# Keys as the moving operand, exp(S) as the stationary one, in a decode-attention and MLP kernel

## The chip, the cores and the metric

The kernel runs on one core of a Trainium2 chip. The metric is device time in microseconds (us), the median of several executions. A run is called slow when it lies over 1.5% above the fastest run of the same kernel. PE is TensorE's matmuls, PEld its weight loads, DVE VectorE, ACT ScalarE, POOL GpSimd, SP the engine that issues the loads. The granted clock is the share of TensorE's full clock that the profile records as let through; half clock is a share of 0.5.

## The reference

One decode step for four sequences: attention over a window of 2048 cached keys and values, and an MLP branch on the same input. Cut to what matters:

```python
# B=4, D=576, Hq=32, Hkv=16, Dh=128; the last W=2048 of 8192 cached positions
xn = layernorm(x)
q  = xn @ wq                                            # 576 x 4096
s  = einsum(q, k_cache[:, :, -W:]) * Dh**-0.5           # two query heads share one K/V head
o  = einsum(softmax(s), v_cache[:, :, -W:]) @ wo        # 4096 x 576
... # B: x1 = xn + (shifted gelu branch; with S=1 the shift leaves zeros)
h2 = gelu(layernorm(x1) @ w3) @ w4                      # 576 x 4608, 4608 x 576
out = x + o + x1 + h2
```

All inputs are bf16. The kernel must read 87.17 MB from HBM: 16 heads with 2.10 MB of K and 2.10 MB of V each, and wq, wo, w3 and w4.

## The kernel before

For each K/V head it loads K and V whole. VectorE transposes K in 32x32 blocks, four calls a head. TensorE then takes the transposed keys as the stationary operand (loaded into the array) and streams the queries past them. V is the stationary operand of P*V. The eight columns are four sequences times two query heads.

```python
def k_scores(h, s):                       # a quarter of a head: 4 groups x 4 matmuls of 32 columns
    kt = kts.pop((h, s))[:].bitcast(BF16)
    for g in range(SC // NQD):
        for ie in range(4):
            nc.tensor.matmul(out=S_ps[h][:, ...], lhsT=kt[:, ib, ...], rhs=qz[:, h, ib, e]..., ...)

def pv(h, s):                             # 16 matmuls of 8 columns, V stationary, and 2 of ones for the sums
    for g in range(CG):
        nc.tensor.matmul(out=O_ps[h][:, 0:NJ], lhsT=vn[:, g * NQD + s, :], rhs=pt[:, g, s, :], ...)
    ...

for t in range(Hkv):                      # hm = t-1: softmax; hv = t-2: P*V
    for s in range(NSL):                  # four steps
        k_transpose(t, s)                 # VectorE
        if s == 0: sm_max(hm), o_norm(hv - 1)
        elif s == 2: o_pick(hv - 1)       # VectorE's part of the output projection
        pv(hv, s)
        if s == 0: k_mask(t)
        k_scores(t, s)
        if s == 0: sm_maxT(hm)
        elif s == 1: sm_sub(hm), 16 x sm_exp, o_spread(hv - 1)   # spread: every fourth head
        elif s == 3: o_proj(hv - 1)                              # projection: every fourth head
        if t == G_AT: mlp_g(...)          # MLP-up, at t = 7
    flush_loads()                         # issue the loads whose buffers come free
```

Loads go out in the order of use: wq, K0, K1, K2, V0, K3, V1, K4, V2, w3, K5, and so on, w4 last. A load waits for one of seven K/V buffers.

## Time and profile before

| | before |
|---|---|
| time, median | 215.49 us (215.28 to 215.77) |
| span of the profiled run | 213.3 us |
| read from HBM | 87.17 MB |
| busy: PE, DVE, ACT | 57%, 56%, 33% |

These lines of the page of the kernel before give the span, the granted TensorE clock and the DMA share in 40 slices of equal length (a digit is a tenth), the GB/s of each slice, and two DMA queues with their packets, MB and share of 16 engines' time.

```profile
span 213.3 us, 6449 instructions
PEclk9999999999999999999999999999999999999998
DMA  7999999999999999999999999999999999999970
GB/s 247 433 427 418 436 422 430 436 430 418 442 414 429 436 433 420 438 427 430 427 430 430 421 433 425 433 424 427 432 433 421 425 436 424 430 427 419 423 303 29
q1 hardware_dynamic: 6788, 87.17, 96.3%
q8 instruction: 22, 0.36, 0.6%
```

The loads never pause. The next lines are the end of the chain of waits (start, duration, what): the last K, then w4, then the last 16 matmuls and a copy. Nothing but loads holds the end.

```profile
151.57 31.14 DMA kn<-in_A_k_cache_dram
182.73 26.91 DMA w_sb<-in_B_w_dram
209.68 0.46 PE acc L266 x16
210.16 0.31 DVE fin L489
```

Two groups of matmuls by shape (count, busy us, mean ns of one): 512 columns take 601 ns, 144 columns 298 ns.

```profile
L277 PE MATMUL S<-negbig,ohT 4*128 4x512 bf16 x16 | 9.6, 601 | 0.0
L266 PE MATMUL acc<-w_sb,gT 128*32 128x144 bf16 x144 | 4.7, 298 | 1.7 <-DMA w_sb<-in_B_w_dram 1.6
```

### The profile page before, as it was taken

How to read it: one execution, taken by the hardware profiler on the slowest of the kernel's cores; microseconds unless marked ns; L12 is line 12 of the kernel's file. 1: busy time of each engine (PE TensorE's matmuls, PEld its weight loads, DVE VectorE, ACT ScalarE, POOL GpSimd, SP SyncE). 2: the span in 40 equal slices, each digit the busy share in tenths (PEclk: the TensorE clock that was granted, in tenths of full speed). 3: DMA queues.
4: the chain of work that ended last, by engine and by line, in shares of the span. 5: the costliest groups of instructions: out<-in, count | busy, mean ns of one | idle time of the engine just before them, and what ended most of it. 6: DMA issues, size and time to landing. Idle time of an engine off the chain costs nothing. (4 is left out here: it accounts for less than half of the span.)

```text
span 213.3 us, 6449 instructions
## 1 busy us (share of the span) xinstructions
PE 121.1 (57%) x2893; PEld 95.6 (45%) x2893; DVE 119.2 (56%) x223; ACT 70.4 (33%) x258; POOL 8.1 (4%) x18
## 2 busy tenths in 40 slices
PE   0261256757470017157999477786474704869782
PEld 0260133545360015145899365564453603647671
DVE  4708799867470037348610798895664732956120
ACT  0000003681634002608070035670816250618700
POOL 4600300000000000000000000000000000000000
PEclk9999999999999999999999999999999999999998
DMA  7999999999999999999999999999999999999970
GB/s 247 433 427 418 436 422 430 436 430 418 442 414 429 436 433 420 438 427 430 427 430 430 421 433 425 433 424 427 432 433 421 425 436 424 430 427 419 423 303 29
DMA packets 6822, 87.57 MB, mean 410 GB/s; under 512 B 776, under 2 KB 780, under 8 KB 1292
## 3 DMA queue, kind: packets, MB, share of 16 engines
q1 hardware_dynamic: 6788, 87.17, 96.3%
q8 instruction: 22, 0.36, 0.6%
q14 instruction: 4, 0.03, 0.0%
q10 hardware_dynamic: 8, 0.00, 0.0%
HBM read 87.17 MB, written 0.00 MB: 409 GB/s over the span
## 5 line engine op out<-in xcount | busy, mean ns | idle before, releaser
L314 ACT ACTIVATE pt<-S 32x128 bf16<-32x128 f32 x256 | 68.8, 269 | 90.9 <-issue 55.0
L196 DVE STREAM_TRANSPOSE kt<-kn 128x1024 int32<-128x1024 int32 x64 | 74.6, 1208 | 11.6 <-DMA kn<-in_A_k_cache_dram 11.6
L325 PE MATMUL O<-pt,vn 128*128 128x8 bf16 x1024 | 37.5, 169 | 41.9 <-DMA vn<-in_A_v_cache_dram 40.4
L325 PEld LDWEIGHTS <-vn 128*128 128x128 bf16 x1024 | 34.5, 105 | 49.9 <-DMA vn<-in_A_v_cache_dram 42.1
L285 PE MATMUL S<-qz,kt 128*128 128x32 bf16 x1024 | 39.1, 189 | 25.7 <-DVE kt L196 25.7
L285 PEld LDWEIGHTS <-kt 128*128 128x128 bf16 x1024 | 33.6, 106 | 36.6 <-DVE kt L196 30.9
L299 DVE TENSOR_REDUCE m<-mxT 8x1 f32<-8x128 f32 x16 | 4.4, 277 | 41.0 <-PE mxT L297 41.0
L328 PE MATMUL O<-pt,ones_bf 128*128 128x64 bf16 x128 | 17.1, 226 | 0.0
L314 ACT ACT_TABLE_LOAD x1 | 1.3, 1283 | 33.3 <-DVE mx L292 33.3
L377 PEld LDWEIGHTS <-w_sb 128*128 128x128 bf16 x144 | 11.4, 163 | 0.5 <-issue 0.4
L377 PE MATMUL AB<-ln2T,w_sb 128*128 128x4 bf16 x144 | 11.5, 202 | 0.0
L292 DVE TENSOR_REDUCE mx<-S 128x8 f32<-128x512 f32 x16 | 10.5, 654 | 1.0 <-PE S L285 1.0
L307 PE MATMUL S<-dg,ones_bf 8*128 8x512 bf16 x16 | 9.6, 601 | 0.1
L277 PE MATMUL S<-negbig,ohT 4*128 4x512 bf16 x16 | 9.6, 601 | 0.0
L328 PEld LDWEIGHTS <-ones_bf 128*128 128x128 bf16 x128 | 8.4, 104 | 0.0
L379 PE MATMUL AB<-ln2T,w_sb 128*128 128x4 bf16 x36 | 7.3, 202 | 0.0
L336 DVE TENSOR_REDUCE dn<-O 128x8 f32<-128x64 f32 x16 | 3.3, 209 | 5.5 <-PE O L328 5.5
L384 DVE COPY g_x<-AB 128x144 f32<-128x144 f32 x1 | 0.3, 307 | 10.7 <-PE AB L379 10.7
L297 PE MATMUL mxT<-ident_f,mx 128*8 128x128 f32 x16 | 6.0, 374 | 0.3 <-DVE mx L292 0.3
L379 PEld LDWEIGHTS <-w_sb 128*128 128x128 bf16 x36 | 5.9, 163 | 0.0
L266 PE MATMUL acc<-w_sb,gT 128*32 128x144 bf16 x144 | 4.7, 298 | 1.7 <-DMA w_sb<-in_B_w_dram 1.6
L266 PEld LDWEIGHTS <-gT 128*32 128x32 bf16 x144 | 3.8, 130 | 2.4 <-issue 2.2
(76 smaller groups left out, 68.8 us busy)
## 6 DMA issues: line engine op xcount, KB each, us to landing
kn<-in_A_k_cache_dram SPq DMA_DIRECT2D x16, 2048.0 KB, 29.6
vn<-in_A_v_cache_dram SPq DMA_DIRECT2D x16, 2048.0 KB, 26.9
wo_sb<-in_A_wo_dram SPq DMA_DIRECT2D x4, 1152.0 KB, 29.0
w_sb<-in_B_w_dram SPq DMA_DIRECT2D x2, 2304.0 KB, 32.9
wq_sb<-in_A_wq_dram SPq DMA_DIRECT2D x2, 2048.0 KB, 9.5
w_sb<-in_B_w_dram SPq DMA_DIRECT2D x2, 1440.0 KB, 31.7
w_sb<-in_B_w_dram SPq DMA_DIRECT2D x3, 576.0 KB, 30.4
w_sb<-in_B_w_dram SPq DMA_DIRECT2D x1, 1152.0 KB, 31.7
```

The source lines that it names most:

```text
L196: nc.vector.transpose(out=kt[:], in_=src)
L266: nc.tensor.matmul(out=acc[i * QD:(i + 1) * QD, :], lhsT=lhsT, rhs=rhs[:, i * CW:(i + 1) * CW], start=False, stop=False, skip_group_check= ...
L277: nc.tensor.matmul(out=S_ps[h][:].rearrange("p g k j -> p (g k) j"), lhsT=ohT[:], rhs=nb, start=True, stop=False, skip_group_check=True)
L285: nc.tensor.matmul(out=S_ps[h][:, s * (SC // NQD) + g].rearrange("p k j -> p (k j)"), lhsT=kt[:, ib, g * NQD:(g + 1) * NQD, e:2 * QD:2].re ...
L292: nc.vector.reduce_max(out=mx[:], in_=S_ps[h][:].rearrange("p g k j -> p j (g k)"), axis=AX.X)
L297: nc.tensor.transpose(out=mxT[:], in_=st[h][:], identity=ident_f[:])
L307: nc.tensor.matmul(out=S_ps[h][:].rearrange("p g k j -> p (g k) j"), lhsT=ones_bf[0:NJ, :], rhs=dg, start=False, stop=False, skip_group_ch ...
L314: nc.scalar.activation(out=PT[h][kb * QD:(kb + 1) * QD, :, c4, :], in_=S_ps[h][c4 * QD:(c4 + 1) * QD, :, kb, :], func=ACT.Exp, scale=scale)
L325: nc.tensor.matmul(out=O_ps[h][:, 0:NJ], lhsT=vn[:, g * NQD + s, :], rhs=pt[:, g, s, :], start=(g == 0 and s == 0), stop=False, skip_group ...
L328: nc.tensor.matmul(out=O_ps[h][:, NJ:].rearrange("p (c j) -> p c j", j=NJ), lhsT=ones_bf[:], rhs=pt[:, g:g + DG, s, :], start=False, stop= ...
L377: nc.tensor.matmul(out=g_ps[:, i, :], lhsT=w3[:, j * F + e * (F // 2) + f0:j * F + (e + 1) * (F // 2):NFH], rhs=ln2T[:, j, :], start=False ...
L379: nc.tensor.matmul(out=g_ps[:, i, :], lhsT=w3[:, KJ * F + f0:KJ * F + F // 2:NFH], rhs=ln2T[:, KJ + e, :], start=False, stop=False, skip_g ...
```

## The change

Swap the operands. The queries, placed in a block of zeros, become stationary, and 512 keys at a time stream past them: 16 score matmuls a head instead of 64. exp(S) is turned by VectorE and becomes the stationary operand of P*V, with 512 columns of V moving: 16 matmuls instead of 64, in four column groups of the array. q and MLP-up are made wide in the same way. ScalarE needs one exponential per head instead of 16. The core of the diff:

```diff
-NKV = 7
+NKV = 6
-    CW = D // NQD          # projections in 4 column groups of 144
+    CW = D // 2            # 2 column groups of 288
     def k_scores(h, s):
-        for g in range(SC // NQD):
-            for ie in range(4):
-                nc.tensor.matmul(out=S_ps[h][...], lhsT=kt[...], rhs=qz[:, h, ib, e]...)
+        for ie in range(4):
+            nc.tensor.matmul(out=S_ps[h][:], lhsT=qz[:, z0:z0 + P], rhs=kt[:, ib, :, e:2 * QD:2]..., ...)
+    def sm_turn(h):  nc.vector.transpose(out=PT[h][:], in_=E.pop(h)[:])
+    def sm_den(h):   # row sums: one matmul, then a reciprocal on VectorE
-    def pv(h, s):  ... lhsT=vn[:, g * NQD + s, :], rhs=pt[:, g, s, :]     # 64 + 8 sums a head
+    def pv(h):     ... lhsT=pt[:, c, :], rhs=vn[:, :, c, :]               # 16 a head
+    def o_scale(h):  # ScalarE copies O times 1/sum;  o_turn(h): 4 transposes on TensorE, a reduction
     ...
         for s in range(NSL):
             k_transpose(t, s)
+            if s == 0: sm_max(hm), o_turn(hf), k_mask(t)          # hf = t - 3
             k_scores(t, s)
             if s == 0: sm_maxT(hm)
-            elif s == 1: sm_sub(hm), 16 x sm_exp(hm), o_spread(hv - 1)
-            elif s == 3: o_proj(hv - 1)      # and o_pick at s == 2
+            elif s == 1: sm_sub(hm), sm_exp(hm), o_spread(hf)     # with o_pick inside it
+            elif s == 2: o_proj(hf)
+            elif s == 3: sm_turn(hm), sm_den(hm), pv(hv), o_scale(hv)
```

Where both kernels do a step with different tiles, the cut shows only the call. The setup grows too: q is copied and transposed back, and the zeroed query block is four times as large.

## The prediction

> **What bounds the kernel now.** The loads. The page's queue table gives 87.17 MB from HBM at a busy share of 96.3%; the 40 slices show 418 to 442 GB/s from the second slice to the last but two, with no dip. The chain of waits ends in DMA (35% of the span, PE 2%, DVE 2%): its last links are the last K (landed at 182.7 us), the MLP-down weights (209.6), 0.46 us of matmuls, a 0.31 us copy and about 2.8 us of output. Per head the loads need 4.19 MB, about 9.8 us at 430 GB/s.
>
> **What the change does.** Bytes stay the same. Per head, estimates from durations in the trace:
> - TensorE before: 64 score and 64 P*V matmuls at about 33 ns start to start, 8 sums, mask and subtraction at 0.53 us each: about 6 us.
> - After: 16 score matmuls of 512 columns. The groups by shape give 168 ns for 8 columns, 298 for 144, 602 for 512: 0.83 ns a column. The Trainium skill (TensorE: Matmul & The Clock Gate, Part 1) has 1.2 GHz for an idle array, 2.4 GHz after about 3.4 us of sustained work; this trace shows only the slow rate. The scores are then 6.8 us slow or 3.5 us fast; P*V, four column groups at once, 1.8 or 0.9; mask, subtraction, transposes 1.5 to 2. Sum: 10.3 us slow, 6 us fast: fewer instructions, not less TensorE time. I expect the dense streams to raise the clock at least partly.
> - ACT: 4.3 to about 1.4 us.
> - DVE: the K transposes stay, the turn of exp(S) adds about 0.6 us: 6.4 to about 7 us.
> All this lies off the critical path.
>
> **What could reach the path.**
> 1. Start. The q chain grows: the first K transpose moves from 26.9 us to about 32 (estimate). With six K/V buffers instead of seven, six loads cover the queue until about 45.5 us (summed bytes). The seventh needs the first K released, at about 37 us; the eighth the second K, at about 46, and it is needed by about 48. Probably no gap, else 1 to 3 us.
> 2. End. The final projections use two column groups of 288 in place of four of 144: per weight tile about 240 ns slow, against 130. The last two pieces of MLP-down then end 0.3 to 1.1 us later after the same landing; the split copy returns 0.1.
> 3. Instruction fetch (0.6% of DMA time) shrinks to a third: at most 0.8 us back.
>
> **Predicted time:** 216.0 us, range 214.8 to 219.0. Chances: faster by over 2% 0.02, within 2% 0.86, slower by over 2% 0.12.
>
> **What would show the steps right.** Slices: DMA at 9 throughout, no dip at 45 to 55 us. The chain of waits: still K, V and MLP-down loads. The 512-column score matmuls at about 600 ns (slow clock) or 380 (fast). PE instructions a third, PE busy not. First K transpose near 32 us. Last piece of MLP-down landing within 1 us of 209.6, then 1 to 2 us of matmuls.
>
> **What would make it wrong.** If the clock stays slow, an iteration (scores in four steps, each behind a K transpose, the maximum and subtraction between) takes about 12 us against 9.8; buffers come back late, DMA shows gaps, and the time could reach 225 to 240. A later start (first K transpose beyond 35 us) leaves a gap at about 50 us. Faster would need a higher HBM rate.

## The result, and the profile after

The change is slower: 226.74 us median of four runs, two fast (224.66, 224.69) and two slow (228.78, 231.47). The ratio to the kernel before is 1.0427, 95% interval 1.0407 to 1.0447. A ratio is the mean time of one kernel's fast runs over that of the other's of the same rounds, so it is not quite the ratio of the medians. The outputs are correct. The run shown here is a fast one.

The same lines of the page of the changed kernel:

```profile
span 222.9 us, 2388 instructions
PEclk9999555995969999979995599958999996699589
DMA  6999999999999999999999999999999999999000
GB/s 239 429 441 435 432 421 441 425 426 429 426 420 436 444 412 435 438 435 426 429 429 426 438 426 426 435 432 432 400 405 439 438 426 429 418 431 399 16 0 2
q1 hardware_dynamic: 6778, 87.17, 92.1%
q8 instruction: 7, 0.11, 0.2%
```

The loads ran as fast as before and hardly paused (apart from the first and the last ones, the lowest slices are two near 161 us, with 400 and 405 GB/s), and they ended earlier: the last three slices of the span, 16.7 us, hold next to no data. So no missing buffer starved the loads for long. What follows the loads is new. The last pieces of its chain of waits are all compute (the scaled copy of O, its transposes, P*V of the last head, the projections):

```profile
208.21 0.70 ACT O_sb L379
...
208.95 1.12 PE oT L385 x4
210.07 1.82 PE O L374 x13
211.89 1.97 PE acc L307 x16
...
215.19 4.36 PE acc L307 x68
```

The VectorE transposes of the last head's K started at 193.3 us, 13 us after that K had landed (180.1 us, from the landings in the trace). What followed was late by a similar amount: the last V landed at 195.3 us and its P*V began at 210.0. In a repaired kernel (f1 below), where the same K and V landed at 180.1 and 194.7 us, these steps began at 180.2 and 195.4.

Two groups of the changed kernel by shape. The scores took 449 ns on average, the same mask matmul 398 instead of 601:

```profile
L328 PE MATMUL S<-kt,qz 128*128 128x512 bf16 x256 | 79.6, 449 | 33.4 <-DVE kt L203 33.4
L319 PE MATMUL S<-negbig,ohT 4*128 4x512 bf16 x16 | 6.4, 398 | 0.0
```

### One head at full clock

PE's timeline over one head of the changed kernel (start, duration, what; in brackets the idle time before it and what ended that):

```profile
77.83 0.39 PE L319 MATMUL S<-negbig,ohT 4*128 4x512 bf16 x1
78.15 1.07 PE L328 MATMUL S<-kt,qz 128*128 128x512 bf16 x4
79.15 0.17 PE L341 MATMUL mg<-dm,sel_jb 128*8 128x16 bf16 x1
80.73 1.06 PE L328 MATMUL S<-kt,qz 128*128 128x512 bf16 x4 [1.40 <-DVE kt L203]
81.73 0.39 PE L347 MATMUL S<-nm,j_row 8*128 8x512 bf16 x1
82.04 2.00 PE L328 MATMUL S<-kt,qz 128*128 128x512 bf16 x8
83.88 0.28 PE L363 MATMUL dn<-rs,same_j 128*128 128x1 f32 x2
84.09 1.05 PE L374 MATMUL O<-vn,PT 128*32 128x512 bf16 x16
85.98 0.66 PE L385 MATMUL oT<-ident_w,O_sb 128*128 128x128 f32 x4 [0.84 <-ACT O_sb L379]
86.57 0.39 PE L319 MATMUL S<-negbig,ohT 4*128 4x512 bf16 x1
```

The mask matmul (L319) opens the scores of each head, so the time from mask to mask is the length of a head: 8.74 us. Of these PE waits 1.40 us for the second K transpose and 0.84 us for ScalarE's scaled copy. VectorE over the same stretch shows why the transpose is late: it first waits 1.13 us for PE's result of the maximum (mg), reduces it, and only then starts the three remaining K transposes. At the end of the head it waits for the denominator.

```profile
79.36 0.17 DVE L343 TENSOR_REDUCE nm<-mg 8x1 bf16<-8x16 f32 x1 [1.13 <-PE mg L341]
79.45 3.48 DVE L203 STREAM_TRANSPOSE kt<-kn 128x1024 int32<-128x1024 int32 x3
82.93 0.71 DVE L359 STREAM_TRANSPOSE PT<-E 128x512 bf16<-128x512 bf16 x1
84.20 0.17 DVE L365 RECIPROCAL rd<-dn 128x1 f32<-128x1 f32 x1 [0.56 <-PE dn L363]
```

### A head with the output projection

Every fourth head also projects: matmuls spread the outputs of four heads into a wider block (R), VectorE picks each one's part out of it, and matmuls with wo follow. In PE's timeline of the changed kernel, the third group of scores waits 2.19 us for its K transpose, because VectorE first waits for R and picks from it; the projection's 16 matmuls then stand before the last scores, at half the clock.

```profile
90.78 0.37 PE L400 MATMUL R<-on,sel_wo 128*128 128x32 bf16 x8
93.34 1.45 PE L328 MATMUL S<-kt,qz 128*128 128x512 bf16 x4 [2.19 <-DVE kt L203]
94.72 2.10 PE L307 MATMUL acc<-wo_sb,op 128*32 128x288 bf16 x16
96.75 1.28 PE L328 MATMUL S<-kt,qz 128*128 128x512 bf16 x4
```

The start of the maximum on VectorE, once a head, gives the length of each head. From the fifth head on (start at 75 to 77 us), read from the timelines of VectorE; P marks heads with a projection, M the one with MLP-up:

```
us per head             P      M                    P                           P  sum of ten
before       10.60  13.93  21.65   6.12   6.77   8.50   8.38   9.72  10.29  14.69       110.7
after         8.84  13.88  19.68  10.62   8.68  14.94   9.12   8.36   8.74  14.84       117.7
```

In the kernel before, long heads wait for loads (TensorE waits 40.4 us for V in all) and short ones catch up. In the changed kernel no head after the start waits for a load: it is simply behind. Repaired versions, shown below, that do wait for the loads need 105.6 us for these ten heads, so the changed kernel loses 12.1 us here. The three projection heads take 43.7 us, the MLP head 19.7, the six others 54.4.

### The profile page after: what moved, and what is told of

Same layout as the page of the kernel before. It is cut to its first block, busy times and chain, and to the rows that moved or that the text cites. A ratio compares the mean times of both kernels' runs of the same rounds, so it can differ in the third digit from the quotient of the medians.

```text
span 222.9 us, 2388 instructions
## 1 busy us (share of the span) xinstructions
PE 148.8 (67%) x955; PEld 63.0 (28%) x955; DVE 134.1 (60%) x230; ACT 26.5 (12%) x56; POOL 13.7 (6%) x20
## 5 line engine op out<-in xcount | busy, mean ns | idle before, releaser
L328 PE MATMUL S<-kt,qz 128*128 128x512 bf16 x256 | 79.6, 449 | 33.4 <-DVE kt L203 33.4
L328 PEld LDWEIGHTS <-qz 128*128 128x128 bf16 x256 | 24.7, 105 | 69.9 <-issue 56.3
L353 ACT ACTIVATE E<-S 128x512 bf16<-128x512 f32 x16 | 9.6, 597 | 97.9 <-PE S L347 97.9
L385 PE MATMUL oT<-ident_w,O_sb 128*128 128x128 f32 x64 | 11.0, 296 | 12.0 <-ACT O_sb L379 12.0
L374 PE MATMUL O<-vn,PT 128*32 128x512 bf16 x256 | 18.4, 411 | 0.0
L379 ACT ACTIVATE O_sb<-O,rd 128x512 f32<-128x512 f32 x16 | 11.0, 687 | 61.3 <-issue 43.4
L365 DVE RECIPROCAL rd<-dn 128x1 f32<-128x1 f32 x16 | 2.7, 166 | 23.2 <-PE dn L363 23.2
L359 DVE STREAM_TRANSPOSE PT<-E 128x512 bf16<-128x512 bf16 x16 | 11.2, 701 | 3.1 <-ACT E L353 3.1
L385 PEld LDWEIGHTS oT<-ident_w,O_sb 128*128 128x128 f32 x64 | 7.0, 145 | 19.7 <-ACT O_sb L379 19.5
L391 DVE TENSOR_REDUCE on<-oT 128x8 bf16<-128x128 f32 x16 | 4.7, 291 | 12.1 <-PE oT L385 12.1
L334 DVE TENSOR_REDUCE mx<-S 128x1 f32<-128x512 f32 x16 | 10.5, 656 | 1.4 <-PE S L328 1.4
L175 DVE TENSOR_SCALAR first<-first,mv,rstd 4x576 bf16<-4x576 bf16 x2 | 8.1, 4074 | 1.4 <-POOL rstd L174 1.4
L307 PE MATMUL acc<-wo_sb,op 128*32 128x288 bf16 x64 | 7.5, 405 | 0.0
L319 PE MATMUL S<-negbig,ohT 4*128 4x512 bf16 x16 | 6.4, 398 | 0.0
```

The source lines that it names most:

```text
L175: nc.vector.tensor_scalar(out=dst_bf[:], in0=src[:], scalar1=mv[:, 0:1], scalar2=rstd[:, 0:1], op0=ALU.subtract, op1=ALU.mult)
L307: nc.tensor.matmul(out=acc[i * QD:(i + 1) * QD, :], lhsT=lhsT, rhs=rhs[:, i * CW:(i + 1) * CW], start=False, stop=False, skip_group_check= ...
L328: nc.tensor.matmul(out=S_ps[h][:], lhsT=qz[:, z0:z0 + P], rhs=kt[:, ib, :, e:2 * QD:2].rearrange("p c k -> p (c k)"), start=False, stop=Fa ...
L334: nc.vector.reduce_max(out=mx[:], in_=S_ps[h][:], axis=AX.X)
L353: nc.scalar.activation(out=E[h][:].rearrange("p c k -> p (c k)"), in_=S_ps.pop(h)[:], func=ACT.Exp, scale=scale, accum_out=rs[:])
L359: nc.vector.transpose(out=PT[h][:], in_=E.pop(h)[:])
```

## The experiments

The first theory (chain theory): the loop is a serial chain over VectorE and TensorE that is longer than the loads, from the first head on, so its waits and a late start reach the end. Its rivals: the half-rate stretches of TensorE's clock (clock theory), and the sixth buffer in place of the seventh (buffer theory).

### e1: the denominator one head later

```diff
             elif s == 3:
-                sm_turn(hm); sm_den(hm)
+                sm_turn(hm)
             if s == 0: sm_maxT(hm)
+                       sm_den(hv)
```

> The change's kernel with the denominator (row sums matmul and reciprocal on VectorE) issued one head later, so that VectorE no longer waits for it in front of the next K transpose; same work. Chain theory (from the first head on, the loop is a serial chain over VectorE and TensorE that is longer than the loads, so its waits reach the end): VectorE's 23 us of waits at the reciprocal go, the head period at full clock falls from 8.74 to about 7.5 to 8 us, and the time falls from 224.7 by 5 to 9 us, to 216 to 220. Clock theory (the half-rate stretches of TensorE are the cause): under 2 us. Buffer theory (six K/V buffers instead of seven starve the loads): under 2 us.

Measured: 229.31 to 230.58 us in three fast runs (a slow one took 233.26), ratio 1.0677. This expectation failed. The longest waits of VectorE (us in total, times, longest) in this run:

```profile
DVE on L391 <- PE oT L385: 24.2, 15, 3.8
DVE nm L343 <- PE mg L341: 14.7, 15, 1.1
DVE mx L334 <- PE S L328: 10.2, 8, 2.9
```

The 23.2 us of waiting at the reciprocal went, but the waits came back at the next operations that need PE (in the changed kernel the lines of `on` and `mx` had 12.1 and 1.4 us). So the long wait was not a link of the chain; VectorE waited there because PE was behind. From P*V to P*V a head at full clock took 8.87 us against 8.73. Why the time rose by 5 us is only partly settled: the denominator's matmul and reciprocal now stand between the maximum and the second transpose, and 0.14 us a head makes 2 us. The clock record holds 34.1 us of half clock in the ten heads of the table above, against 27.3 in the changed kernel, which can be part of the rest; no run separates it.

### e2: the pick and the projection later in the head

```diff
     def o_spread(h): ...                 # the matmuls only
+    def o_pick(h): ...                   # VectorE's part
             k_transpose(t, s)
+            if s == 2: o_pick(hf)
-            elif s == 2: o_proj(hf)
             elif s == 3:
                 ... pv(hv); o_scale(hv)
+                o_proj(hf)
```

> The change's kernel with the output projection's parts put where the kernel before had them: VectorE picks at step 2 instead of at once behind the matmuls of step 1, and the projection matmuls come last in step 3 instead of before the third scores. Chain theory: the three head periods with a projection in the loop (13.9 to 14.9 us against 8.7) fall to about 11, so 216 to 220 us. Clock theory: a gain only as far as half-rate stretches vanish with it. Buffer theory: no change.

Measured: 213.25 us, ratio 0.9902 (0.9886 to 0.9919). This one placement undoes the whole loss, and more. The projection heads fell to 12.35, 11.24 and 10.26 us, 9.8 us less in all.

### e3: idle matmuls where TensorE waits

```diff
+    def keep_busy(n):   # n matmuls of 512 columns into an unused bank
             if s == 0: sm_maxT(hm); keep_busy(4)
             elif s == 1: ... o_spread(hf); keep_busy(6)   # in heads with a projection
             elif s == 3: ... o_scale(hv); keep_busy(3)
```

> The change's kernel with 7 idle matmuls of 512 columns per head (13 where a projection is) into an unused PSUM bank, placed where TensorE waits. Clock theory: the record shows full clock through the loop and the time falls by more than 5 us, to below 219. Chain theory: the clock stretches go, but they were worth 1.5 to 2 us each in four to six heads, so 2 to 5 us less at most, perhaps offset by the idle matmuls' own 0.9 us where they do not fit the gap; 220 to 225.

Measured: 214.45 us, ratio 0.9954 (0.9939 to 0.9969). So the clock theory's number was met, and the chain theory's 2 to 5 us were too small. The row of the granted clock in this run, with two half-rate stretches left between the start and the tail:

```profile
PEclk9999555899999979999999699999999999999589
```

The projection heads took 12.34, 12.36 and 12.36 us, the MLP head 18.48. The order of the other instructions is the same; the matmuls of these heads now ran at full clock.

### e4: the kernel before with six buffers

```diff
-NKV = 7
+NKV = 6
```

> The kernel before with six K/V buffers instead of seven, nothing else. Chain and clock theory: as before, 215.0 to 216.5 us. Buffer theory: 220 us or more.

Measured: 215.29 us, ratio 0.9993 (0.9978 to 1.0008). The buffer theory falls, as far as the kernel before goes; in the changed kernel the nearly unbroken DMA row says the same, though no run gives it a seventh buffer.

The sums for ten heads show how e2 and e3 can each be enough:

```
us                  3 projection heads   MLP head   6 others   ten heads
after                     43.7             19.7       54.4       117.7
e2 pick late              33.9             18.4       56.1       108.3
e3 idle matmuls           37.1             18.5       53.0       108.5
f1 transpose ahead        36.0             19.7       49.9       105.6
```

The least that any run here took under the loads is 105.6. The excess of 12.1 us is small against the work, and either cause, placement or clock, accounts for most of it. They are coupled: in the changed kernel a half-clock stretch begins in or right behind the stall of each of the three projection heads (at 93.8, 145.0 and 186.0 us). Only e3 changes the clock alone. In e2 the second and third projection heads also hold less half clock, 3.4 and 0 us instead of 6.8 each, so a part of their gain is the clock's.

### f1: the second K transpose ahead of the maximum

```diff
         for s in range(NSL):
-            k_transpose(t, s)
+            if s != 1: k_transpose(t, s)
             ...
             k_scores(t, s)
+            if s == 0: k_transpose(t, 1)
             if s == 0: sm_maxT(hm)
```

> The change's kernel with the second K transpose of each head issued to VectorE ahead of the reduction of the maximum, so that TensorE's 1.40 us wait in front of the second scores should go. Chain theory, mended after the first runs (the chain runs through TensorE: scores, maximum, second K transpose, scores, P*V, scaling on ACT, transposes, next scores): the head period at full clock falls from 8.74 to about 7.5 us and the time from 224.7 to 213 to 217, as far as the loads allow. If that wait lies off the chain, as the denominator's did, nothing changes or it gets slower.

Measured: 212.82 us, ratio 0.9880 (0.9865 to 0.9895). PE's timeline of this run, one head:

```profile
129.55 0.39 PE L319 MATMUL S<-negbig,ohT 4*128 4x512 bf16 x1
129.87 1.07 PE L328 MATMUL S<-kt,qz 128*128 128x512 bf16 x4
130.88 0.17 PE L341 MATMUL mg<-dm,sel_jb 128*8 128x16 bf16 x1
131.16 1.06 PE L328 MATMUL S<-kt,qz 128*128 128x512 bf16 x4
...
137.17 0.39 PE L319 MATMUL S<-negbig,ohT 4*128 4x512 bf16 x1
```

The 1.40 us wait is gone, and mask to mask is 7.62 us. So the chain does run through this wait: the four heads without extra work that ran wholly at full clock in both kernels (8.68, 9.12, 8.36 and 8.74 us before this edit) each fell by 1.1 us.

The clock is not ruled out by this run. Its mean (0.866) is no better than in the changed kernel (0.862), but the half-clock stretches lie elsewhere. In the changed kernel the second and third projection heads hold 6.8 us of half clock each; here they hold none, and their projection ran at full clock:

```profile
PEclk9999555896999859658999959999999999996588
143.56 1.16 PE L307 MATMUL acc<-wo_sb,op 128*32 128x288 bf16 x16
```

These two heads fell by 3.9 and 3.5 us. In e3 the clock alone took 2.6 and 2.5 us off them. So, as an estimate, up to about 5 of the 12.1 us that f1 won came with the clock and the rest from the shorter chain. That the clock is not the whole cause is shown by the four heads at full clock, and by the first projection head in e2: with 3.4 us of half clock, as in the changed kernel, it took 12.35 instead of 13.88 us. The mended chain theory holds, and the pure clock theory falls; but the shorter chain did not bring the time back with the clock unchanged.

### f2: an earlier start

```diff
+    # constants, xsum and the second layernorm on VectorE, before the q chain
     q_ps = [...]                         # q matmuls, copies, transposes as before
-    # the same, after the q chain
```

> The change's kernel with VectorE's work on constants and on the second layernorm, which does not need q, issued before the q chain, in 5.8 us in which VectorE waits for q. First K transpose at about 27 instead of 32.6 us. Chain theory: the loop never waits for loads, so nearly all of it reaches the end: 218 to 220.5 us. If the loads or the buffers paced the loop: under 1 us.

Measured: fast runs 225.00 and 226.33 us, slow 231.11 and 231.13; ratio 1.0476. The first K transpose moved from 32.6 to 24.1 us and nothing came of it. The chain theory's claim about the start was wrong, and VectorE's waits on loads in this run (a slow one; the wait stands before its slow part) say why:

```profile
DVE kt L203 <- DMA kn<-in_A_k_cache_dram: 12.7, 1, 12.7
```

The fifth K after the first lies behind w3 in the queue. The maximum that follows its first transpose starts at 75.4 to 75.8 us in e2, e3, f1, f2, g1 and g2, whatever the start; in the changed kernel at 76.7. Of the 5.7 us of later start all but 1.1 were therefore paid back before the loop began to lose.

### f3: four column groups in the projections

```diff
-    CW = D // 2
+    CW = D // NQD
-        for i in range(2): matmul(acc[i * QD:...], ...)
+        for i in range(NQD): matmul(acc[i * QD:...], ...)
```

> The change's kernel with the output projection and MLP-down in four column groups of 144 columns again, as before the change, and the final copy as before. The 44 weight tiles of the end took about 6.9 us of TensorE in two groups; in four I expect about 5. In the loop 1 us less in each of three heads. Chain theory: 220 to 223 us. If only the clock mattered: 224 to 225.

Measured: 222.64 us median, fast runs 221.84 to 222.86; ratio 1.0336. As expected, a small part of the loss, about 2 us.

### f4 and g3: more instructions in the kernel before

The loads of the changed kernel end 2 us earlier than before, which the prediction had not foreseen. A load is done when each of the 16 DMA engines has done its step. The times of these 16 steps for the last piece of w4, from the landings in the trace (us):

```
before  205.0 205.1 205.3 205.3 205.3 205.4 206.3 206.8 208.1 208.2 208.3 209.4 209.5 209.6 209.6 209.6
after   205.9 205.9 206.1 206.1 206.1 206.2 206.2 206.3 206.5 206.7 206.7 206.7 206.9 206.9 207.0 207.6
```

Before, some engines finish 4.6 us after others. A theory for it: the fetch of instructions occupies some of them. To test it, idle one-element memsets on POOL were added to the kernel before, 2000 of them first.

```diff
+    for _ in range(2000):                # 1200 in g3
+        nc.gpsimd.memset(idle[:], 0.0)
```

> The kernel before with 2000 one-element memsets added on GpSimd, which is idle there, so about 0.13 MB more instructions to fetch. Fetch theory (instruction fetch occupies some of the 16 DMA engines, so that the steps of one load land up to 4.6 us apart, and fewer instructions bring the last landing forward from 209.6 to 207.6 us): the last step of the last load lands 1 to 2 us later than 209.6 and the time rises to 216.5 to 217.5. If fetch does not matter: 215.3 to 215.8.

Measured: 322.38 us. I had mis-sized the memsets: POOL was still working through them long after the loads, so the time says nothing. The landings do: one step of the last piece came at 213.0 us, the others by 209.7. Hence the repetition with 1200.

> The kernel before with 1200 one-element memsets on GpSimd: at the 0.145 us each that the run with 2000 showed, they end before the loads do, which that run missed. That run's last load had one of its 16 steps at 213.0 us, the others at 209.7 or earlier. Fetch theory: again one late step, 1 to 2.5 us behind the others, so 216 to 218. If fetch does not matter: 215.3 to 215.8.

Measured: 218.34 us, ratio 1.0135 (1.0120 to 1.0150), 0.3 us above the range expected of the time. The steps of the last piece of w4:

```
g3      205.2 205.2 205.3 205.4 205.6 206.5 207.5 208.0 208.1 208.3 209.6 209.6 209.6 209.8 209.9 212.7
```

One engine is 2.8 us behind the rest, and the time rose by 2.8 us (218.34 less 215.54, the median before in the same rounds). The page of g3 counts 14 packets of instruction fetch on POOL's queue (q14) where the kernel before has 4; the ten more took 3.3 us together in the trace, enough for the delay if one engine served them all, which the trace does not tell. So adding instructions to an idle engine made a load-bound kernel slower, most likely by their fetch; that the running memsets themselves held an engine up was not tested. That the changed kernel's earlier landing comes from its 4061 fewer instructions fits this; it was not tested by adding to the changed kernel.

### g1 and g2: the repairs together

g1 joins e2, f1 and f3; g2 adds f2.

> The change's kernel with three repairs together: the pick late, the second K transpose ahead of the maximum, four column groups in the projections. Slack theory (each repair alone only has to bring the loop back under the loads' pace; the rest is then hidden): no sum of the gains; the last landing stays at 207 us and the time is 212.2 to 213.0, about 0.3 us under the second-K-transpose run, from the shorter end. If gains added up: below 210.

> The same with the earlier start too. Slack theory: equal to the run with three repairs within 0.4 us, since the loop waits for the fifth head's K load (about 75 us) whenever it started. If the start counted: 2 us less or more.

Measured: 212.65 us for both, ratio 0.9872 (0.9858 to 0.9887) for both, outputs correct. The gains do not add, and the start still counts for nothing. The last piece of w4 landed at 207.0 us in both. These are the fastest kernels, 1.3% under the kernel before, with f1 alone (0.9880) within their interval: one moved line is worth nearly all of it.

### g4: idle matmuls in the kernel before

```diff
             k_scores(t, s)
+            for _ in range(4):           # 240 columns into unused PSUM columns
+                nc.tensor.matmul(out=AB[:, (Hq + NF) * B:512], lhsT=ident_bf[:], rhs=qz..., ...)
```

> The kernel before with four idle matmuls of 240 columns after each group of scores, into unused PSUM columns. It tells whether the kernel before ran at half clock although its record says 0.995: if so, the 512-column mask falls from 602 to about 380 to 400 ns in part of the heads and clock changes appear in the record; the time stays within 1 us of before, since the loads bound it. If the record of before was right, the mask stays at 602 ns.

Measured: 223.14 us, ratio 1.0376: the time was expected within 1 us of before and rose by 7.6. The question of the clock is answered all the same. The mask of 512 columns (duration in ns, least, median, most):

```profile
L277 PE MATMUL S<-negbig,ohT x16: 384/602/603, 26.8 to 196.5; 4*128 4x512 bf16 x16
```

384 or 385 ns now appears where the record of this run reports full clock, and 602 where it reports half (0.62 on average); the one exception is the first mask, 584 ns at 26.8 us, before any change was recorded. In the kernel before every 512-column matmul of the loop takes 581 to 603 ns, and its record holds one change only, near the end. The 144-column matmuls of its last stretch fall from 328 to 223 ns there, at about 208 us. So the kernel before ran at half clock nearly throughout; the digit 9 in its PEclk row stands for time in which no change was recorded. The time of g4 also repeats the case in small: the loads land by 209.9 us, as before, but the heads are now too long for the loads' pace, and the tail starts late.

## Why the prediction was wrong

- "What bounds the kernel now. The loads." Right: more of TensorE's work at half clock was hidden under them, and six buffers cost nothing (e4).
- "Sum: 10.3 us slow, 6 us fast: fewer instructions, not less TensorE time." The direction was right (PE busy 148.8 us against 121.1 with a third of the matmuls), and the rate too: 512 columns took 384 or about 600 ns, as the clock stood. The Trainium skill (TensorE: Matmul & The Clock Gate, Part 1) has two clock rates, 1.2 and 2.4 GHz; in the changed kernel four scores in a row took 1.07 us at full clock and 1.87 us at half. The kernel before had shown the fast rate too, in its last matmuls of 144 columns.
- "All this lies off the critical path." This is the step that failed. I added up the busy time of each engine and compared each sum with the 9.8 us of the loads. A head is a chain across engines: 8.74 us at full clock, with 2.24 us of waits between PE, VectorE and ScalarE in it (f1 removed 1.1 us of a head, and the loss went, in part through the clock). And the heads with a projection and with MLP-up were not sized at all: 13.9 to 14.9 and 19.7 us. Their excess is what the loads' slack could not hold (e2). I had considered a long head only for a clock that stays slow.
- "I expect the dense streams to raise the clock at least partly." Right, yet the partial drops mattered: keeping it up was worth about 10 us (e3).
- "DMA shows gaps" as the sign of a late loop. Not the sign at this size of delay: the loads kept their pace but for about 0.6 us (last landing 207.6 us, 207.0 in g1 and g2), and the backlog of 13 us appeared as compute behind the last landing. The loads' row alone would have passed as healthy. Real gaps appear only in later loops: e1 has one slice at 313 GB/s and its last landing at 209.2 us. That the measured time lies in the "225 to 240" of this paragraph is luck: the clock did not stay slow, and a head at full clock took 8.74 us, not 12.
- Start: the first K transpose near 32 us (32.6) and no gap at 45 to 55 us: right. It would not have mattered (f2).
- End: "0.3 to 1.1 us later after the same landing". Wrong in both parts. The last landing came at 207.6 us, 2 us earlier, probably since fetch does not cost "at most 0.8 us" averaged over 16 engines but delays single engines (g3; not tested on the changed kernel). And 12 us of matmuls followed it because the last head was late, not because of the column groups, which were worth about 2 us (f3).

So the sum: the last landing came 2.0 us earlier (207.6 against 209.6), and the last matmul ended 11.9 us behind it (219.5) instead of 0.5 us (210.1). That is 9.4 of the 9.6 us by which the span grew.

## What to carry to other kernels

Under a load-bound loop, compare the loads' time per iteration with the length of the whole chain across engines, for the ordinary iterations and for those with extra work, not with any engine's busy sum; the slack is spent once, and an excess appears at the end, behind loads that look nearly perfect. The longest wait on an engine need not be in the chain (e1); the one to remove is a wait of the engine that works through the chain, and moving one line in the program order can do it (f1). Several causes that each use up a common slack each look like the whole cause when repaired alone, so their gains must not be added.

## What the Trainium skill lacked or had wrong

- TensorE: Matmul & The Clock Gate, "Why this matters for your kernels", asks for no idle gaps over about 3 us between bursts of matmuls. In the loop of the changed kernel no gap between matmuls was longer than 2.35 us, and the clock still fell to half six times, for 3.4 to 10.2 us each. So this row's limit did not keep the clock up here; no run gives the limit that would.
- The same page warns of clock records that can't be trusted, but not that a record without changes can be read as full clock: 0.995 in the kernel before, where 512 columns took 602 ns.
- The same page, "Back-to-back issue gap", gives about 131 ns per matmul of 512 columns in a sustained stream. Four score matmuls took 1.07 us with 387 ns for the last of them, so about 228 ns each (in a run of four only); its figure for isolated ones, about 216 ns, is nearer.
- Runtime: NRT & Kernel Launch, "Instruction fetch mechanics", calls the cost of a new 16 KiB block of instructions mostly hidden. For the load-bound kernel of g3 it was not: with 1200 idle instructions on POOL one of 16 DMA engines was 2.8 us behind, and the time rose by 2.8 us.
- SBUF — State Buffer, "SBUF: two separate sides", describes the port pair that VectorE and GpSimd share as an exclusive lock. The changed kernel fits it: a VectorE layernorm step of 4x576 elements took 7.02 us beside a 6.93 us memset on GpSimd, against 1.88 us beside one of 1.79 us before. The page could add that the profile shows such a block as a long instruction, not as a wait.
